# Nine matmuls fewer in batch 0 of a fused attention and MLP kernel, and batch 0's six up-products in one slot

## Chip, cores, metric

One core of a Trainium2 chip. The metric is device microseconds (us) of one execution. The profile of an execution is the record of one such run; its span is some 1.7 us shorter than the time. A difference of 0.1% is 0.3 us here, so the whole case is about tenths of a microsecond in 310.

## The reference

Sliding-window causal attention (8 batches, 8 heads, 576 positions, head size 64, window 64), then a low-rank mix over the positions and a two-layer MLP. Cut to what matters:

```python
rel = pos[:, None] - pos[None, :]
mask = (rel >= 0) & (rel < 64)
attn = softmax(where(mask, q @ k.T / 8, -1e9))      # 8 batches x 8 heads, 576 x 576
x = (attn @ v) -> [8, 576, 512]
u = x + ((x.T @ U) @ V).T                           # U: 576 x 32, V: 32 x 576
out = u + relu(u @ w_ch1) @ w_ch2                   # 512 -> 2048 -> 512, fp32 in and out
```

## The kernel before

Matmuls are bf16. The attention of batch 0 runs first, alone ("prologue"). After that come nine chunks of 512 tokens, each cut into 32 slots: 16 of the first MLP product (tile psA, weights w1b) and 16 of the second (psU, weights w2b). The attention of batches 1 to 7 is cut into pieces that tables place into these slots, so that PE, the tensor engine, never runs dry. `spare` is true for batch 0 alone.

Batch 0's scores, with the product that the change drops: key block 1 against query block 0, where every key lies in the future.

```python
        def SC(j):                       # one head pair
                ...
                scores(banks, 0, j, 0, 0, 2)
                scores(banks, 0, j, 1, 0, 1)
                for u in range(1, NB - 1):
                    scores(banks, u, j, u, u, 2 if u < NB - 2 else 1, last=(u >= NB - 3))
```

The up-products multiply the 64 rank rows (`hh`) by V (`vrep`) into tile psv; the vector engine adds the attention output and so makes u in token-major order:

```python
        def VM(ts, banks=None):          # -> [up, add(0), add(1)]
            def up():
                ...
                for n in range(2):
                    ...
                    nc.tensor.matmul(ps[0][n], vrep[half, off : off + P], hh["sb"][half, lo : lo + cols], start=True, stop=True)
        ...
            pcs["V"] = [f for ts in ((0, 1), (2, 3), (4,)) for f in VM(ts)]     # batch 0
    ...
    DVE_RELU = {0: (7, 9, 11, 15), 1: (3, 6, 8, 9, 10, 12, 13)}
    PLACE_0 = {"V": [0, 0, 1, 2, 2, 3, 4, 4, 4]}
    PLACE_2 = {"S": [8, 8, 8, 11, 11], "M": [8, 9, 10, 12, 13], ...}
```

The first batch is number 0. Batches 2 to 7 get their keys and queries in three steps: GpSimd issues the loads (kr, qr), SyncE (SP) issues ten loads that transpose them (kf, qf) and PE multiplies. Of such a transfer the text names three times: its issue by SP, its landing (the data are there), and its first use. PLACE_2's "S" puts batch 2's scores behind slot 8 of chunk 1. GpSimd waits for a transposed tile before it loads the next batch into the same place:

```python
            def loads(b, *tiles):
                for t in tiles:          # a one-element copy, to wait for transposed tile t
                    nc.gpsimd.tensor_copy(out=held[:], in_=qfs[(b + 1) % 2][0:1, t * HP * P : t * HP * P + 1])
                if b <= 2:
                    load_v(b + 1)
                for _ in load_kq(b + 2, False): pass
            ...
            if b == 1:
                slots[20].append(lambda: loads(1, 2))
```

The prologue begins with matmuls that compute nothing and warm PE up, and has one more of the kind, 512 columns wide, before the third values block:

```python
    turn_over(62, 96)                    # 62 matmuls of 96 columns into an unread bank
    ...
    shift_low(0, nc.scalar.copy, 2)
    a["idle"](1)
    a["PV"][2]()
```

The softmax here doesn't subtract the row's maximum and nothing guards it: scores larger than these inputs give would overflow.

## Time and profile before

| | before |
|---|---|
| time, first 3 runs | 310.14 us (309.88 to 310.33) |
| span of the profiled run | 308.6 us |
| PE busy | 302.1 us, 98% |
| start of the third values block of batch 0 | 16.28 us |
| first psA of chunk 0 | 22.02 us |
| slot 22 of chunk 0 (needs the last quarter of w2b) | 48.45 us, worked out in the prediction |
| first score of batch 2 | 67.59 us |

The lines of the page, the chain and the timeline are in the prediction.

In the chain of waits of before (start, length, what), PE stands still in the middle of the U products:

```profile
19.53 0.32 PE psh L534 x2
19.85 0.31 issue
20.16 0.32 PE psh L543 x4
```

And SP's timeline of before (start, length of the issue, queue, operation, tiles) has the ten transposing loads of batch 2; here the third and the last:

```profile
51.62 1.58 SPq L307 DMA_TRANSPOSE kf<-kr  x1
...
61.52 1.22 SPq L307 DMA_TRANSPOSE qf<-qr  x1
```

The last takes this long to land after its issue:

```profile
DMA to landing us min/median/max: 5.5/5.5/5.5
```

So batch 2's last queries are there at 61.52 + 5.5 = 67.0 (67.06 in the trace), and PE uses them at 67.59. A margin of half a microsecond, as narrow as the ones that the prediction counted at 33, 46 and 48 us.

### The profile page before, as it was taken

What the parts mean: (1) busy time and instruction counts of PE and PEld (TensorE: products, weight loads), DVE (VectorE), ACT (ScalarE), POOL (GpSimd) and SP (SyncE); (2) the same over time, 40 slices, a digit from 0 to 9 for tenths busy, and PEclk for the clock granted to TensorE, in tenths of its full rate; (3) what the DMA queues carried; (4) which work ended last, traced back from release to release, by engine and by line L of the source; (5) the groups of instructions that cost most, each with busy time, mean ns of one, the idle gap of its engine ahead of it and who ended that gap; (6) DMA issues with size and microseconds to landing.
All of it is one profiled execution on the core that took longest, in us unless ns stands there. A gap on an engine that the chain in (4) does not pass through costs nothing.

```text
span 308.6 us, 6947 instructions
## 1 busy us (share of the span) xinstructions
PE 302.1 (98%) x2883; PEld 146.4 (47%) x2883; DVE 174.2 (56%) x336; ACT 106.0 (34%) x169; POOL 102.1 (33%) x136
## 2 busy tenths in 40 slices
PE   7989999999999999999999999999999999999995
PEld 7543454545445544454445444544454444444443
DVE  4585467537848763777467755766576542116012
ACT  2745670358008510552064205430443004101500
POOL 8693264195069519417541725000000000000000
PEclk9999999999999999999999999999999999999999
DMA  7999999999999999999999999955100464010011
GB/s 100 169 208 209 206 172 149 148 139 148 148 108 154 126 158 148 195 161 163 175 176 131 176 175 151 155 111 136 71 2 0 106 229 162 34 68 36 0 68 68
DMA packets 158671, 40.39 MB, mean 131 GB/s; under 512 B 147216, under 2 KB 153616, under 8 KB 158640
## 3 DMA queue, kind: packets, MB, share of 16 engines
q0 software_dynamic: 104720, 18.88, 84.8%
q1 hardware_dynamic: 53920, 21.08, 39.3%
q8 instruction: 22, 0.36, 0.5%
q14 instruction: 9, 0.07, 0.1%
HBM read 37.97 MB, written 9.44 MB: 154 GB/s over the span
## 4 chain that ended last, share of the span: by engine, by line
PE 93%; DMA 3%; POOL 2%; issue 1%; DVE 0%; POOLq 0%
PE psA L766 41%; PE psU L790 41%; DMA vA<-in_v_dram 3%; PE sc L348 3%; PE xw L410 2%; PE psv L661 1%; PE pshh L534 1%; PE tpg L284 0%; POOL qr L121 0%; PE low L348 0%; PE psh L534 0%; POOL vB L153 0%; PE tpu L695 0%; PE xr L410 0%; POOL kr L121 0%
## 5 line engine op out<-in xcount | busy, mean ns | idle before, releaser
L766 PE MATMUL psA<-uTc,w1b 128*128 128x512 bf16 (+1 forms) x580 | 131.0, 378 | 0.3 <-DVE uTc L636 0.3
L790 PE MATMUL psU<-w2b,c 128*128 128x512 bf16 (+2 forms) x592 | 128.4, 374 | 0.0
L790 PEld LDWEIGHTS <-c 128*128 128x128 bf16 x592 | 56.1, 98 | 66.4 <-issue 2.9
L766 PEld LDWEIGHTS <-w1b 128*128 128x128 bf16 x580 | 54.0, 98 | 64.4 <-issue 2.6
L778 ACT ACTIVATE c<-psA 128x512 bf16<-128x512 f32 x84 | 50.1, 597 | 80.5 <-PE psA L766 80.2
L776 DVE TENSOR_SCALAR c<-psA 128x512 bf16<-128x512 f32 x60 | 41.4, 690 | 38.5 <-PE psA L766 38.5
L803 DVE TENSOR_TENSOR osb<-psU,un 128x512 f32<-128x512 f32 (+2 forms) x29 | 19.5, 671 | 51.2 <-PE psU L790 51.2
L368 ACT ACTIVATE pts<-sc 128x1024 bf16<-128x1024 f32 x32 | 31.3, 1030 | 2.8 <-PE sc L348 2.8
L139 POOL DMA_DIRECT2D vA<-in_v_dram x32 | 28.3, 904 | 11.5 <-DMA w1b<-in_moe_w_ch_dram 3.0
L676 DVE TENSOR_TENSOR un<-psv,xs 128x512 bf16<-128x512 f32 (+3 forms) x48 | 25.8, 594 | 6.6 <-PE psv L661 6.5
L130 POOL DMA_DIRECT2D qr<-in_q_dram x30 | 26.6, 887 | 7.0 <-DMA w2b<-in_moe_w_ch_dram 2.9
L130 POOL DMA_DIRECT2D kr<-in_k_dram x30 | 26.3, 876 | 5.0 <-PE psA L766 2.0
L401 ACT ACTIVATE ptl<-low 128x256 bf16<-128x256 f32 x6 | 2.3, 383 | 64.9 <-PE high L348 64.9
L374 DVE TENSOR_TENSOR pts<-pts,maskA 128x1024 bf16<-128x1024 bf16 x28 | 19.0, 683 | 2.2 <-ACT pts L368 2.2
L501 DVE TENSOR_TENSOR xs<-xw,rcw 128x896 bf16<-128x896 f32 x14 | 15.3, 1092 | 0.5
L965 POOL COPY held<-qf 1x1 bf16<-1x1 bf16 x5 | 0.9, 178 | 44.2 <-DMA qf<-qr 44.2
L348 PEld LDWEIGHTS <-kf 64*64 64x64 bf16 x704 | 9.8, 107 | 7.6 <-issue 7.3
L348 PE MATMUL sc<-qf,kf 64*64 64x128 bf16 (+1 forms) x608 | 11.5, 212 | 0.5 <-DVE qf L301 0.3
L410 PEld LDWEIGHTS <-pts 128*64 128x64 bf16 x512 | 10.0, 110 | 3.7 <-issue 3.1
L139 POOL DMA_DIRECT2D vB<-in_v_dram x8 | 7.2, 896 | 5.6 <-DMA qr<-in_q_dram 2.4
L803 DVE TENSOR_TENSOR late<-psU,un 128x512 f32<-128x512 f32 x8 | 5.4, 686 | 6.1 <-PE psU L790 6.1
L410 PE MATMUL xw<-vA,pts 128*64 128x65 bf16 x217 | 8.5, 195 | 0.0
(125 smaller groups left out, 177.1 us busy)
## 6 DMA issues: line engine op xcount, KB each, us to landing
out_dram<-osb SPq DMA_DIRECT2D x27, 256.0 KB, 2.3
vA<-in_v_dram POOLq DMA_DIRECT2D x32, 128.0 KB, 9.6
kr<-in_k_dram POOLq DMA_DIRECT2D x24, 128.0 KB, 7.6
qr<-in_q_dram POOLq DMA_DIRECT2D x24, 128.0 KB, 7.5
w2b<-in_moe_w_ch_dram POOLq DMA_DIRECT2D x4, 512.0 KB, 15.6
out_dram<-late SPq DMA_DIRECT2D x8, 256.0 KB, 3.0
vB<-in_v_dram POOLq DMA_DIRECT2D x8, 128.0 KB, 11.3
w1b<-in_moe_w_ch_dram POOLq DMA_DIRECT2D x2, 512.0 KB, 10.9
```

Of the source, the lines that this page charges most:

```text
L130: nc.gpsimd.dma_start(out=dst[0:rows, t, :, :], in_=src[b, :, t * P : t * P + rows, :].rearrange("h p d -> p h d"),)
L139: nc.gpsimd.dma_start(out=dst[:, :, 0:D], in_=v[b, :, lo : lo + P, :].rearrange("h p d -> p h d"))
L348: nc.tensor.matmul(sc[g][r0 : r0 + W, col * W : (col + n) * W], keys_of(j, u, rs), queries_of(j, blk, n, rs), start=not spare, stop=last o ...
L368: nc.scalar.activation(out=dst, in_=sc[:], func=ACT.Exp, scale=scale)
L374: nc.vector.tensor_tensor(out=dst, in0=dst, in1=maskA.rearrange("p g n w -> p g (n w)"), op=ALU.mult)
L410: nc.tensor.matmul(dst, pts[:, h // 2, h % 2, blk, :] if blk < NB - 1 else ptl[:, h // 2, h % 2, :], rhs, start=True, stop=True,)
L676: nc.vector.tensor_tensor(out=u_tiles[g][rs, cs], in0=ps[0][n][rs], in1=x[rs, t, :, :].rearrange("p h d -> p (h d)")[:, cs], op=ALU.add,)
L766: nc.tensor.matmul(ps[i][:, ts.start * P : ts.stop * P], w1b[:, dc, i * P : (i + 1) * P], uTc[:, ts, dc, :], start=(dc == 0), stop=(dc == ...
L776: nc.vector.tensor_relu(out=c1[i][:], in_=ps[i][:])
L778: nc.scalar.activation(out=c1[i][:], in_=ps[i][:], func=ACT.Relu)
L790: nc.tensor.matmul(acc[t][:, lo:hi], c1[i][:, t * P : (t + 1) * P], w2b[:, i, lo:hi], start=(i == 0), stop=(i == NFC - 1),)
L803: nc.vector.tensor_tensor(out=osb[:, lo:hi], in0=acc[t][:, lo:hi], in1=u_tiles[g][:, lo:hi], op=ALU.add,)
```

## The change

The intent: drop work that cannot matter (eight score products under the mask, one idle matmul), and pay PE's change of array shape once for the six up-products instead of three times.

```diff
-                scores(banks, 0, j, 1, 0, 1)
+                if not spare:
+                    scores(banks, 0, j, 1, 0, 1)
...
-        def idle_turns(n):               # and its users
...
-            pcs["V"] = [f for ts in ((0, 1), (2, 3), (4,)) for f in VM(ts)]
...                                       # two_banks and mixed are now defined for every batch
+        if spare:
+            pcs["V"] = [lambda: mixed([VM((NT - 1,), two_banks), VM((0, 1)), VM((2, 3))])]
...
-    DVE_RELU = {0: (7, 9, 11, 15), 1: (3, 6, 8, 9, 10, 12, 13)}
+    DVE_RELU = {0: (9, 11, 15), 1: (3, 6, 8, 9, 10, 12, 13)}
...
-    PLACE_0 = {"V": [0, 0, 1, 2, 2, 3, 4, 4, 4]}
+    PLACE_0 = {"V": [4]}
...
-    a["idle"](1)
```

Each of the nine matmuls has a weight load beside it: the trace of before shows 2883 of both, 5766 rows of PE's instruction stream. The change takes out 18.

More of the change, by code (lines that the diff above doesn't have):

```diff
@@ L590, in bank @@
             return ua[dc]
-        opened = []
-        def idle_turns(n):
-            cols = P if opened else CH
-            bank(1)
-            for _ in range(n * (CH // cols)):
-                nc.tensor.matmul(
-                    bank(0)[:, 0:cols],
-                    idle[:, 0:P],
-                    idle[:, 0:cols],
-                    start=not opened,
-                    stop=not opened,
-                )
         def XT(t, dcs):
             def f():
-                opened.append(t)
                 for dc in dcs:
@@ L716, in attention, with two_banks, mixed, last @@
             pcs["XT"] = [XT(t, range(NDC if t < 2 else 2)) for t in range(NFULL)]
-            pcs["idle"] = idle_turns
             pcs["X3"] = [XT(t, (2, 3)) for t in (2, 3)]
             pcs["HT"] = [HT((0, 1)), HT((2, 3))]
-            pcs["V"] = [f for ts in ((0, 1), (2, 3), (4,)) for f in VM(ts)]
-        else:
-            def two_banks():
-                return (
-                    psum["mm"].tile([P, CH], FP32, name="psv0", tag="mm"),
-                    ps_tp.tile([P, CH], FP32, name="psv1", tag="tp"),
-                )
-            def mixed(parts=None):
-                parts = parts or [VM((0, 1)), VM((2, 3)), VM((NT - 1,), two_banks)]
-                for part in parts:
-                    part[0]()
-                for part in parts:
-                    for add in part[1:]:
-                        add()
-            pcs["V"] = [mixed]
-            if b == 1:
-                def last():
-                    for f in VM((NT - 1,)):
-                        f()
-                pcs["V"] = [lambda: mixed([VM((0, 1)), VM((2, 3))]), last]
+        def two_banks():
+            return (
+                psum["mm"].tile([P, CH], FP32, name="psv0", tag="mm"),
+                ps_tp.tile([P, CH], FP32, name="psv1", tag="tp"),
+            )
+        def mixed(parts=None):
+            parts = parts or [VM((0, 1)), VM((2, 3)), VM((NT - 1,), two_banks)]
+            for part in parts:
+                part[0]()
+            for part in parts:
+                for add in part[1:]:
+                    add()
+        pcs["V"] = [mixed]
+        if spare:
+            pcs["V"] = [lambda: mixed([VM((NT - 1,), two_banks), VM((0, 1)), VM((2, 3))])]
+        if b == 1:
+            def last():
+                for f in VM((NT - 1,)):
+                    f()
+            pcs["V"] = [lambda: mixed([VM((0, 1)), VM((2, 3))]), last]
+        if not spare:
             pcs["UT"] = [UT(t) for t in range(NT if odd else NT - 1)]
         return pcs
-    DVE_RELU = {0: (7, 9, 11, 15), 1: (3, 6, 8, 9, 10, 12, 13)}
+    DVE_RELU = {0: (9, 11, 15), 1: (3, 6, 8, 9, 10, 12, 13)}
     DVE_RELU_N = (0, 1, 2, 4, 5, 6, 14)
```

## The prediction

> **What bounds the kernel now.** I read the page first, then the chain of waits in order of time, then the timeline around the places that the change touches. The page gives the bound: the tensor engine (PE) is busy for 98% of a span of 308.6 us and makes up 93% of the chain that ended last; the granted clock is full in every slice.
>
> ```profile
> PE 302.1 (98%) x2883; PEld 146.4 (47%) x2883; DVE 174.2 (56%) x336; ACT 106.0 (34%) x169; POOL 102.1 (33%) x136
> PE 93%; DMA 3%; POOL 2%; issue 1%; DVE 0%; POOLq 0%
> ```
>
> A PE at 98% does not say that any matmul taken away is time gained: what counts is whether it stood on the chain. The chain, start and length in us, splits the kernel at 16.28 us.
>
> ```profile
> 6.17 8.05 DMA vA<-in_v_dram
> 14.27 0.61 POOL vB L153
> ...
> 15.61 0.62 POOL vB L153
> 16.28 0.45 PE xr L410 x16
> ...
> 22.02 1.89 PE psA L766 x8
> 23.91 0.32 PE psv L661 x2
> 24.23 0.97 PE psA L766 x4
> 25.20 0.32 PE psv L661 x2
> 25.52 1.83 PE psA L766 x8
> 27.36 0.22 PE psv L661 x2
> 27.57 6.15 PE psA L766 x28
> ...
> 83.25 0.65 PE psv L661 x6
> 83.89 5.29 PE psU L790 x24
> ```
>
> Before 16.28 the chain is not PE at all: the load of batch 0's values has to land, and GpSimd then copies them, half a tile at a time, into the shifted layout vB; the last of its four copies runs 15.61 to 16.22 and releases the third block of attention-times-values. From 22.02 on it is PE without a hole worth the name. So a matmul that ends before 16.28 is free, and one after 22.02 is paid for.
>
> The timeline around 16 us shows one of the matmuls that go, and the wait behind it:
>
> ```profile
> 15.61 0.61 POOL L153 COPY vB<-vA 64x520 bf16<-64x520 bf16 x1
> 15.70 0.39 PE L598 MATMUL uam<-idle 128*128 128x512 bf16 x1
> 16.28 0.19 PE L410 MATMUL xr<-vB,pts 128*64 128x65 bf16 x1 [0.19 <-POOL vB L153]
> ```
>
> The last column is what ended PE's idle time: the copy on GpSimd, not PE's own work.
>
> **What the Trainium skill says.** (1) "TensorE: Matmul & The Clock Gate", section "Wait — 56ns, not 53.3ns?": back-to-back bf16 matmuls of 512 columns start 215.7 ns apart at full clock. The trace agrees: late in the chain, 64 of them take 13.81 us, 215.8 ns each. (2) "TensorEngine Tiling (Array Packing)", section "Key Properties": "Changing tiling mode (not just tile) drains the TensorE". The trace agrees and gives a price: four psA take 0.97 us right behind a psv group, where 4 x 0.2158 = 0.86, so 0.11 us is lost on entering the 128-row shape; 8 take 1.83 against 1.73, and 28 take 6.15 against 6.04: 0.11 us each time. (3) The first page again, section "What's actually happening": the clock is held back only after an idle window of some 3.4 us. Nothing here comes near: with the idle matmul gone, PE would rest from about 15.77 to 16.28, 0.5 us. (4) "PSUM — Partial Sum Buffer", section "The four PSUM rules": a matmul that opens a group overwrites, later ones add. In batch 0 every score bank is opened by the mask bias over all its columns, so leaving out scores that the mask drives to zero still leaves defined sums. This bears on correctness, not on time.
>
> **The change part by part.**
>
> *Eight score matmuls.* For each of four head pairs the product of key block 1 with query block 0 is dropped for two heads: 8 matmuls of 64 columns, wholly under the mask. They lie in groups of 18 that last 0.42 us each with a tail of about 0.2, so one is worth some 0.013 to 0.03 us and all eight 0.1 to 0.25 us of PE time, at 9.6 to 14.2 us. None is on the chain: PE waits there for query copies (0.30 us before 9.60, 0.18 before 12.86) and for the query load that releases the transposes at 11.66, and what is left is swallowed by the wait at 16.28. The vector engine runs nearly back to back from 15.88 and could begin a few hundredths earlier, but its next read is of the block released at 16.28. I count 0.00 us, at best 0.05.
>
> *The idle matmul.* One of 512 columns at 15.70, gone by 16.09, 0.19 us before GpSimd lets PE go on. Removing it lengthens that wait: 0.00 us. It also changes which of two PSUM buffers the first transposes take (the idle one opened the other bank first), but both are free long before the end of the copies.
>
> *The up-products.* Before: three groups of two matmuls (512, 512 and 256 columns) with a 64-row weight tile, in slots 0, 2 and 4 of chunk 0. The two of a group use different row halves and run side by side: 0.32 us is 0.216 + 0.11 to change shape. Each group also makes the following psA pay 0.11. Before, in the chain's numbers: 0.32 + 0.32 + 0.22 for the groups and 3 x 0.11 for the psA behind them, 1.19 us. After: all six stand together at the end of slot 4. This kernel already has such a group in batch 2, with the same six shapes: 0.65 us, then 24 matmuls in 5.29 us where 24 x 0.2158 is 5.18, so 0.11 behind it: 0.76 us. Saving: 1.19 - 0.76 = 0.43 us, all after 22.02 and so on the path.
>
> *What moves with it.* The six additions on the vector engine (four of about 0.645 us and two that take 0.74 together, 3.3 us in all) move from 24.27-28.36 to a block that I estimate at 26.8 to 30.1. The relu of slot 7, on the vector engine at 30.38 before, goes to the scalar engine, which has a 0.92 us hole there; the next relu on the vector engine is slot 9's, whose matmuls end at about 31.6 in the new order. The short up-products now take one of the three buffers that the psA of single slots go round in; slot 7 needs it back at about 29.0 and its additions, placed first, should end at about 27.6. Its transposing bank is needed at slot 11, over 5 us later. I expect no wait from any of these.
>
> Sum: 0.00 + 0.00 - 0.43 = -0.43 us of PE chain.
>
> **The rivals.**
>
> *A load takes the place of the saved time.* If PE comes 0.43 us earlier, it can meet a transfer that is bound by bandwidth and does not move: the DMA stays saturated from 5 to 48 us. The last quarter of the second weight is issued at 36.01 after waiting for the first quarter, and lands at 47.97. Its first reader is in slot 22; the 20 psU from 47.48 are slots 21 to 25, so slot 22 begins at 47.48 + 0.11 + 0.86 = 48.45. The margin is 0.48 us now and would be 0.05 after. Batch 1's query load lands at 33.18 against a first use at 33.93 (0.75 before, 0.32 after), and its last value tile at 46.25 against 46.93 (0.68, 0.25). So the gain just fits. For this rival: a landing 0.2 us later in some executions would cost that much, and the total gain cannot pass about 0.48 us by any route before slot 22. It would make the change -0.2 instead of -0.43, a time of 309.9. I give it a third.
>
> *The score matmuls pay after all.* If scores set the start of the values product by way of the exponentials, 0.1 to 0.2 us more would come: -0.6 us, cut to -0.48 by the load above. Against it: the releaser at 16.28 is GpSimd, whose copies wait for value loads alone. One chance in ten.
>
> *Six matmuls in a row stall, or the late additions do.* The group needs its three pairs of PSUM banks at once; if the bank of slot 2's relu or of the first relu pair came late, PE would stand for some tenths, and if the additions ran into slot 9's relu, slot 12 would wait for its buffer. For it: the order of instructions shows such waits on the first two pairs. Against it: the relus of slots 0 to 2 end by about 25.7 by my count, and the group comes at about 26.5. It would make the change -0.1 to +0.3, up to 310.4. One in ten.
>
> *An unexplained stop moves.* At 19.85 PE stands 0.31 us before the last U product, although the vector engine had written its operand by 19.55; the view calls it issue time. If it depends on where instructions lie in the stream, 18 fewer rows may shift, lengthen or cure it: up to 0.3 us either way, the gain again held at 0.48. I cannot tell from one trace.
>
> **Range and chances.** 310.14 - 0.43 = 309.71; a third of a chance of losing about 0.2 to the load adds some 0.05: I say 309.75 us. The three runs before spread from 309.88 to 310.33, so two medians of three may differ by 0.2 with nothing changed; with about the same again for the size of the effect, 8 in 10 is about 0.4 each way: 309.3 to 310.15. Two per cent is 6.2 us, fourteen times the whole effect, and all three groups together cost 1.19: faster by over 2% 0.01, slower by over 2% 0.01, within 0.98.
>
> **What would show it right or wrong.** Right: the third values block still starts at about 16.3, released by the GpSimd copy after an idle of about 0.5 us; the chain has one psv x6 of about 0.65 us near 26.5, with psA groups before it free of the extra 0.11; slot 22's psU start at about 48.0 without a new wait. Wrong: the 16.28 start comes earlier (the scores counted), a hole before psv or before slots 5 to 7 (banks), psU waiting for the second weight at 48 (the load), or the 0.31 stop gone or grown. The prediction fails as a whole if the time leaves 309.3 to 310.15: below it, something earlier than 16.28 or a stall that I don't see was on the path; above it, one of the new waits is real.

## The result, and the profile after

| | before | after |
|---|---|---|
| runs | 310.32 median of 6 (309.88 to 310.58) | 310.91 median of 6 (310.09 to 311.83) |
| profiled run, span | 308.6 | 308.4 |
| ratio after/before | | 1.002, interval 0.9997 to 1.0043 |

A ratio is the mean time of one kernel's fast runs over that of the other's of the same rounds, so it is not quite the ratio of the medians quoted. Executions over 1.5% slower than the fastest of the same kernel are left out of the means.

The six runs of after are 310.09, 310.16, 310.49 and 311.34, 311.47, 311.83: half like before or a little better, half a whole microsecond worse (the last of them at a mean granted clock of 0.994, the others at 0.999 or 1.000). The median, 310.91, lies outside the predicted range. The profiled run is of the better kind (310.09); keep that in mind for the lines that follow.

The page of after, busy times and the chain's shares (some 20 matmul records are missing in this trace, so PE's busy time is a little low and small "issue" gaps in the chain are not real):

```profile
PE 299.4 (97%) x2853; PEld 145.6 (47%) x2874; DVE 175.0 (57%) x335; ACT 106.6 (35%) x170; POOL 101.9 (33%) x136
PE 91%; DMA 3%; DVE 2%; POOL 2%; issue 1%; POOLq 0%; DVEq 0%
```

New there: DVE, the vector engine, with 2% of the chain, where before had 0%. The chain of after, in order of time, says where:

```profile
6.18 8.01 DMA vA<-in_v_dram
...
15.58 0.62 POOL vB L153
16.25 0.45 PE xr L411 x16
...
19.46 0.32 PE psh L535 x2
19.94 0.44 DVE hh L576
...
21.46 4.48 PE psA L753 x20
25.93 0.65 PE psv L647 x6
26.58 6.15 PE psA L753 x28
...
71.96 0.69 DVE c L763
...
97.31 0.69 DVE c L763
...
101.26 0.39 PE xw L411 x13
```

The third values block starts at 16.25, behind the same GpSimd copy (16.28 before). The stop of 0.31 us in the U products is gone; the first psA comes at 21.46 instead of 22.02. The six psv stand together, 0.65 us, and the 28 psA behind them take 6.15 us, the same as before: no stall. At 71.96 and 97.31 the chain leaves PE for the vector engine (c is a relu's output; the copies into vB stand between them and the values product at 101.26).

With matching weight loads of the two traces set side by side, after's lead over before is: 0.03 us at 16.3, 0.57 at 20.4, **0.99 at 27.6** (behind the six psv), 0.89 at 34, **0.70 at 48.3**, **0.54 at 76**, **0.23 at 102.6**, 0.18 from 143.5 to the end. So even in this run of the better kind the change gains 1 us and four fifths of it are given back, in four places: behind batch 1's query load (landed at 32.97, used at 33.02), the last quarter of w2b (48), and twice behind values products that wait for the vector engine (76, 101). What makes half the runs lose is not in this trace. That was the question for the experiments.

### The profile page after: what moved, and what is told of

Read it like the earlier page. It is cut to its first block, busy times and chain, and to the rows that moved or that the text cites. A ratio compares the mean times of both kernels' runs of the same rounds, so it can differ in the third digit from the quotient of the medians.

```text
span 308.4 us, 6907 instructions
## 1 busy us (share of the span) xinstructions
PE 299.4 (97%) x2853; PEld 145.6 (47%) x2874; DVE 175.0 (57%) x335; ACT 106.6 (35%) x170; POOL 101.9 (33%) x136
## 4 chain that ended last, share of the span: by engine, by line
PE 91%; DMA 3%; DVE 2%; POOL 2%; issue 1%; POOLq 0%; DVEq 0%
PE psU L777 40%; PE psA L753 39%; DMA vA<-in_v_dram 3%; PE sc L348 3%; PE xw L411 2%; PE psv L647 1%; DVE c L763 1%; PE pshh L535 1%; DVE pts L375 1%; PE tpg L284 0%; POOL qr L121 0%; PE low L348 0%; PE psh L535 0%; POOL vB L153 0%; PE tpu L681 0%
## 5 line engine op out<-in xcount | busy, mean ns | idle before, releaser
L777 PE MATMUL psU<-w2b,c 128*128 128x512 bf16 (+2 forms) x573 | 127.1, 373 | 1.2 <-issue 0.3
L763 DVE TENSOR_SCALAR c<-psA 128x512 bf16<-128x512 f32 x59 | 40.7, 689 | 37.2 <-PE psA L753 37.2
```

Of the source, the lines that this page charges most:

```text
L763: nc.vector.tensor_relu(out=c1[i][:], in_=ps[i][:])
L777: nc.tensor.matmul(acc[t][:, lo:hi], c1[i][:, t * P : (t + 1) * P], w2b[:, i, lo:hi], start=(i == 0), stop=(i == NFC - 1),)
```

## The experiments

Five calls, each on one chip with its own runs of before beside it. All results were correct. The medians of before in the calls were 310.46, 310.60, 310.49, 310.50 and 310.33 (7 to 11 runs). In what follows "the slower kind" is a run above 310.95 at a mean granted clock of 0.998 or more; the line was drawn after the runs were seen. The theories by their names in the expectations: **H**, the clock (without the nine matmuls PE is granted its full clock less often); the walls, transfers that don't come earlier when PE does; and **R**, the rows (it matters not what the nine matmuls do but that PE's instruction stream is 18 rows shorter). Where another name stands, what it expects tells which of these it is.

### First call: the parts, each alone

**after_again**: the changed kernel, unedited.

> The changed kernel once more, for the spread and the granted clock of each run. In the first set its six runs ranged from 310.09 to 311.83 us, and the 311.83 one had a mean clock of 0.994. Theory H (clock): in some executions the lighter start lets the clock be held back for one stretch; then again some runs above 311 us, and those show a clock clearly below 1.000. Theory C (copies and loads): the lead won early is lost when the vector engine's copies of vA meet GpSimd's issuing of loads; then runs above 311 us appear with a clock of 1.000 too. Theory N (noise of one set): all runs within 309.9 to 310.6 now.

Measured: 309.89, 310.07, 310.11, 311.41, 311.92 and one of 784.85; ratio 0.9995 (0.9956 to 1.0034). In the last, psA took 823 ns each instead of 378. Its trace holds no record of the clock (the 1.000 listed for it stands for that). The two kinds are there again.

**v_only**: before with nothing but the up-products' move and relu 7.

```diff
-            pcs["V"] = [f for ts in ((0, 1), (2, 3), (4,)) for f in VM(ts)]
+            pcs["V"] = [lambda: mixed([VM((NT - 1,), two_banks), VM((0, 1)), VM((2, 3))])]
-    DVE_RELU = {0: (7, 9, 11, 15), ...
+    DVE_RELU = {0: (9, 11, 15), ...
-    PLACE_0 = {"V": [0, 0, 1, 2, 2, 3, 4, 4, 4]}
+    PLACE_0 = {"V": [4]}
```

> The kernel before with only the up-products moved to one slot; the 8 score matmuls and the idle matmul stay. Theory H: no run with a clock below 0.999, times tight (within 0.6 us), 0.0 to 0.4 us faster than before. Theory C: the lead of about 0.43 us is lost partly or wholly by 105 us, as in the changed kernel; times spread as there.

Measured: 309.80 to 310.54, median 310.13, none of the slower kind in 6; ratio 0.9978 (0.9947 to 1.0009).

**no9**: before with nothing but the nine matmuls gone.

```diff
+                if not spare:
-                scores(banks, 0, j, 1, 0, 1)
+                    scores(banks, 0, j, 1, 0, 1)
-    a["idle"](1)
```

> The kernel before without the 9 matmuls, the up-products left in three slots. Theory H: as in the changed kernel some runs 1 us or more above the rest with a clock below 0.999, mean 0.3 to 0.6 us slower than before. Theory C: the early lead is only what the stop at 19.85 us gives back (0.3 us or more, if it is gone here too), so less is lost and times are near those of before, within 0.2 us. My prediction's view of these matmuls (free, off the chain): same time as before within 0.1 us.

Measured: 310.10 to 310.85, median 310.49, none of the slower kind in 6; ratio 0.999 (0.9956 to 1.0024).

**aft_idle**: after with the idle matmul put back.

```diff
+    a["idle"](1)
     a["PV"][2]()
```

> The changed kernel with the one idle matmul of 512 columns back, the 8 score matmuls still gone. Theory H: if that matmul is what kept the clock, no run with a clock below 0.999 and times of 309.7 to 310.2; if the scores matter as well, fewer slow runs but some. Theory C: spread and mean as in the changed kernel, 310.9.

Measured: one run of 619.1 with psA at 671 ns (no clock record either, left out), the others 310.33 to 310.91; ratio 0.9997 (0.9963 to 1.003).

What follows: neither part alone showed the slower kind, but six runs of each are few, and aft_idle, which has both parts but for one matmul, did not show it in five runs either. The clock does not explain it: after's slow runs mostly have a clock of 1.000, and the two clearly held runs of this call, 312.70 and 312.77 at 0.993 and 0.995, are before's own. Theory H fell here.

These two held runs also stand in the ratios of this call. Without them the mean of before is 310.33, and the plain ratios of the means become 0.9994 for v_only, 1.0005 for no9, 1.0012 for aft_idle and 1.0011 for after_again: all nearer to 1.

### Second call: work or rows, and two more looks at after

**less9**: before with nine of the warm-up matmuls fewer, and the nine disputed ones kept. The stream is 18 rows shorter, the prologue's arithmetic untouched.

```diff
-    turn_over(62, 96)
+    turn_over(53, 96)
```

> The kernel before with 53 instead of 62 of the opening matmuls on zeros (0 to 6 us, read by nobody), nothing else: PE's stream is 18 rows shorter ahead of the last U product, all 9 disputed matmuls stay. In the trace of before PE stands 0.31 us ahead of that product (0.56 us against the spacing of the changed kernel, where it follows in 0.14 us), in the trace of v_only 0.10 (0.35), each time starting 1.4 us after a 16 KB packet of the instruction queue ended; in the changed kernel and in no9 the stop is gone. Theory F (the stop is PE waiting for its own instructions, at a fixed row of the stream): the stop is gone here too, the last U product follows the one before within 0.2 us, and the first psA starts 0.4 to 0.6 us earlier than in before. Theory S (the 9 matmuls themselves hold something up): the stop stays at 0.1 to 0.3 us.

Measured: 310.77 to 311.31, ratio 1.0008 (0.9986 to 1.0029). The time decides nothing. The stop in the U products is gone, but PE came late to it (the last U product at 20.19, the first psA at 22.12, against 22.02 in before), so theory F's gain of 0.4 to 0.6 us is not there to be seen. What the trace does show, about another place, stands below.

**no9_plus9**: no9 with nine matmuls of 8 columns put at the very beginning. Nine disputed matmuls gone, rows as before.

```diff
+    turn_over(9, 8)
     turn_over(62, 96)
```

> no9 with 9 matmuls of 8 columns on zeros put ahead of the opening ones, so that PE's rows stand again where they stood in before, without the 9 disputed matmuls. Theory F: the stop ahead of the last U product is back, 0.3 to 0.6 us against a spacing of 0.14, and the first psA starts 0.3 us or more later than in no9. Theory S: the stop stays away and the first psA starts within 0.1 us of that in no9.

Measured: 310.52 to 311.11, ratio 0.9998 (0.9973 to 1.0022). No stop, but PE was late here too (20.42).

Now SP's timelines. In after, the sixth transposing load of batch 2 is the long one, and the last is issued 0.41 us later than in before although the first was issued earlier:

```profile
51.19 1.23 SPq L307 DMA_TRANSPOSE kf<-kr  x1
...
55.28 2.62 SPq L307 DMA_TRANSPOSE qf<-qr  x1
...
61.93 1.22 SPq L307 DMA_TRANSPOSE qf<-qr  x1
```

In less9, too, the lengthened ones are at 55 to 57, with all nine disputed matmuls in place:

```profile
55.20 1.78 SPq L307 DMA_TRANSPOSE qf<-qr  x1
57.08 1.96 SPq L307 DMA_TRANSPOSE kf<-kr  x1
```

In no9_plus9, without those nine but with the rows, it is the third again, as in before:

```profile
51.40 1.86 SPq L307 DMA_TRANSPOSE kf<-kr  x1
```

What lies under it is a transfer of the kind "instruction", one packet of 16,384 bytes. The DMA view of before between 51 and 53 us (kind: packets, MB, share of the engines):

```profile
q8 instruction: 1, 0.02, 3.0%
```

and of after between 55 and 57 us; neither kernel has one in the other's window:

```profile
q8 instruction: 1, 0.02, 5.4%
```

The packets next to it move little (45.77 in before, 45.40 in after; 71.07 and 70.37), this one from 51.81 to 55.28. So theory R holds for the traces: the number of rows moves the packet, whichever matmuls are taken out, and the load that it falls on is long in issue, which delays those behind it. Not all of a long issue is the packet's: the sixth load took 1.57 us in before, with no such packet there.

Set against PE's own work, the place of the packet is sharper than by the clock time. In all nine undisturbed traces of the short stream it starts 0.08 to 0.72 us after the first of PE's transposes of u (tile tpu, 55.04 in after); in all eight of the long stream it starts 3.36 to 4.91 us before it.

**after_look1**, **after_look2**: the changed kernel, to catch the slower kind in a trace.

> The changed kernel, one look, for a trace of the slower of its two kinds of runs: of 11 runs outside the 784.85 us one, 6 took 309.9 to 310.5 and 5 took 311.3 to 311.9 us, four of these at a clock of 0.999 or 1.000. If this look is of the slower kind, its lead over before should be the same 0.9 us or more at 45 us and be lost by 1.3 us more than in the first trace at one place; theory L (loads): at a wait of PE for the second weight or for values, between 40 and 105 us; theory V (vector engine): at the up-products or the values products, behind slow vector copies; theory K: all along, by a lower clock. If it is of the faster kind it tells nothing new.

> A second such look at the changed kernel; the same expectation as for the first: the slower kind of run in about 45 of 100 looks.

Measured: 311.44 and 311.13, both the slower kind. The waits of PE in after_look2 between 66 and 69 us (line, what for: us in all, times, longest):

```profile
PE low L348 <- DMA qf<-qr: 1.2, 1, 1.2
```

That is batch 2's first score, waiting for the last transposed queries. These landed late, by the view of that one load, issued at 61.90:

```profile
DMA to landing us min/median/max: 6.2/6.2/6.2
```

In after's own trace the same load, issued at 61.93, needed 4.9 us and was there at 66.8, just before PE came at 66.90.

In after_look2 PE led before by 1.07 us at 27.6 and 0.69 at 48; behind this wait it was 0.59 *behind* before, and 0.85 behind at the end. after_look1 lost elsewhere: it had started 1.1 us late at 14 to 17, was 0.19 behind from 27.6 to 120, and then stood 0.8 us for batch 4's queries at 126, which landed at 127.32.

So a lead is not only taken back by a wall; the lead can turn into a loss. But there is more than one wall, and PE need not be early to meet one: after_look1 was behind before when it stood at 126.

### Third call: is it the first scores' place?

**after_s9** puts batch 2's scores one slot (0.9 us) later, so that the load is not waited for; **before_s9** is its control. **before_s7** puts before's scores one slot earlier, which makes before use them as early as after does.

```diff
 # after_s9, before_s9 (before_s7 has 7,7,7 and 7,8,9)
     PLACE_2 = {
-        "S": [8, 8, 8, 11, 11],
-        "M": [8, 9, 10, 12, 13],
+        "S": [9, 9, 9, 11, 11],
+        "M": [9, 10, 11, 12, 13],
```

> The changed kernel with batch 2's scores one slot later in chunk 1 (slot 9 in place of 8, masks moved with them). Why: in the second look at the changed kernel PE came to these scores at 66.9 us and stood until 68.18, 0.04 us after the last transposed load of batch 2's queries had landed at 68.14; in its first trace that load landed at 66.83 and PE passed without a wait. Theory T (that load is the wall: PE gains nothing by coming before about 67 to 68 us): PE now comes at about 67.8, the wait is at most 0.4 us, the slower kind of run (311.3 to 311.9 at full clock) is gone, median 309.8 to 310.2, 0.1 to 0.5 us faster than before. Rival V (vector copies behind the values products at 75 and 101 us decide): nothing gained, or 0.3 us lost as masks come later; median 310.8 with the same spread.

Measured: 310.02 to 311.62, median 310.54, ratio 1.0004 (0.9986 to 1.0022). A miss: 309.8 to 310.2 had been expected. In its trace the queries landed at 68.65, later than in any other, and PE waited 0.45 us for them even in the later slot.

> The kernel before with batch 2's scores one slot later, as a control of the move itself: PE comes at about 68.5. Theory T: median within 0.2 us of before, and no run at full clock above 310.8. If the move itself costs (masks later, values products wait at 75 us), it is 0.2 to 0.5 us slower, and that much has to be taken off what after_s9 shows.

Measured: 309.91 to 310.98, median 310.19, ratio 0.9992 (0.9974 to 1.0009).

> The kernel before with batch 2's scores one slot earlier (slot 7 in place of 8), all 9 matmuls and the three-slot up-products in place. PE comes to these scores at about 66.7 us, as early as in the changed kernel. Theory T: the slower kind of run appears in a kernel that has none of the change: some or most runs 0.6 to 1.3 us above before, median 310.6 to 311.6, and the trace shows PE waiting for the load of qf by the transposing queue ahead of the scores. Rival (the slower kind comes from the change's own parts, banks or additions): median within 0.15 us of before, no such wait.

Measured: 309.99 to 311.20, median 310.83, ratio 1.0006 (0.9989 to 1.0022). In its trace the queries landed at 66.26, PE came at 66.38 and had no wait. The median is what theory T expected, but one run of six is of the slower kind and the expected wait was not seen: not decided.

**no9_plus9_b** is the same kernel as no9_plus9, once more for the stop in the U products at 19.85.

> no9_plus9 once more, since in its first look PE came to the last U product only at 20.41 us, later than the time at which its rows were to be expected (the instruction packet ended at 18.90, and 1.43 us later is 20.33). Theory F: if PE comes early this time (the U product before it at 19.4 to 19.8), it stands again until 1.4 us after the packet's end, 0.2 to 0.6 us; if PE is late again it tells nothing.

Measured: 311.44 at a clock of 0.998, and no stop; PE came late into that stretch in both, so they say nothing of it.

### Fourth call: take the company away from the late load

With `loads(1, 3)` GpSimd waits for one transposed tile more before it issues the next values and keys, so that those loads start later and the last transposing load no longer runs beside them.

```diff
-                slots[20].append(lambda: loads(1, 2))
+                slots[20].append(lambda: loads(1, 3))
```

**after_hold3**:

> The changed kernel, with GpSimd holding back the loads of the next batches until the transposed queries of tile 3 of batch 2 have landed, not tile 2. In the traces the last transposed load (tile 4) shares the DMA engines with those value loads and takes 4.9 to 6.4 us from issue to landing (66.3 to 68.7 us), where such loads without that company take 2.4 us. Theory T: it now lands by about 65, PE at 66.9 never waits for it, the slower kind of run is gone (none above 310.8 at full clock), median 309.7 to 310.2, 0.5 to 1.0 us below after_again2. Rival V (later waits behind vector copies take it all back): median within 0.3 us of after_again2, runs above 311 remain.

Measured: 311.10 to 311.46, median 311.26, ratio 1.0022 (1.0007 to 1.0038): a miss in the time. The load itself did what was meant:

```profile
DMA to landing us min/median/max: 2.6/2.6/2.6
```

It landed at 64.56, and PE had no wait at 67. But in the timeline of after_hold3 PE now stands at the first psA of chunk 2:

```profile
92.22 0.38 PE L753 MATMUL psA<-uTc,w1b 128*128 128x512 bf16 x1 [0.84 <-DVE late L790]
```

The releaser that the view names had long been done. It was a transposing load of chunk 2's u, landed at 91.97: SP issued those from 88.20 on, behind batch 3's ten, against 85.82 in before. In this run the wall at 67 was moved to 92, not removed.

**v_only_hold3**, **before_hold3**: the same edit in v_only and in before.

> The up-products alone in one slot, plus the hold; the 9 matmuls stay. Theory T: 309.7 to 310.1, 0.3 to 0.5 us faster than before, all runs within 0.6 us: the up-products' 0.43 us kept for the most part. Rival V: like v_only, 0.1 to 0.3 us faster than before.

Measured: 310.32 to 311.51, median 310.98, ratio 1.0015 (0.9995 to 1.0035); queries landed at 63.85.

> The kernel before with the same hold. PE comes to batch 2's scores at 67.6, in most runs after the landing, so theory T: 0.0 to 0.3 us faster than before, with fewer runs above 310.8. If the hold itself costs (value loads 1.8 us later), it shows here: up to 0.5 us slower.

Measured: 310.03 to 311.45, median 310.91, ratio 1.0008 (0.9987 to 1.0028); landed at 64.04. Three runs of each are of the slower kind, though the nine matmuls are in; before without the edit had 2 of 11 in this call. So the slower kind does not need the short stream, and what the edit gains at 67 can't be read from these times.

**after_again2**: the changed kernel once more, for the count.

> The changed kernel once more, beside after_hold3 on the same chip. Theory T: the slower kind again in about half of the runs, median 310.3 to 311.4; if the trace is of that kind, it shows PE's wait for qf ahead of the scores at 67 to 68 us (or at 126 us, as in the first look).

Measured: 309.99, 310.06, 310.63, 310.73, 311.32 (clock 0.994), 311.44; ratio 1.0004 (0.9984 to 1.0024).

### Fifth call: rows alone

**after_plus9**: after with the rows given back (`turn_over(9, 8)` first, as in no9_plus9).

> The changed kernel with 9 matmuls of 8 columns on zeros put at the very start, so that PE's stream has as many rows as before. Theory R (rows): an instruction packet at 51 to 52 us, none at 55 to 57; the ten transposed loads of batch 2 issued over 12.6 to 12.7 us, the last one about 0.8 us earlier than in the changed kernel; the slower kind of run gone (at most one of six above 310.9 at full clock), median 309.8 to 310.3, at or below before. Theory M (the 9 matmuls or the earlier PE itself): packet and issue as in the changed kernel, slower kind in about half of the runs, median 310.5 to 311.4.

Measured: 309.50, 309.66, 310.55, 310.74, 311.02 and, in the profiled run, 313.27 at a clock of 0.989; ratio 0.9999 (0.998 to 1.0017). Not decided. In that trace the clock was at half from 12.1 to 18.9 us and PE 2 us late everywhere; the packet came at 54.80 and the ten issues took 13.36 us. Its rows are those of before, so R had expected the early packet, at 51 to 52 us. By the clock time that failed; by PE's work it did not: PE came to its first tpu at 57.73 here, and the packet started 2.93 us before that, on the side of the long stream. So PE's lateness goes with the late packet, and the trace speaks for R rather than against it. Of the times, R's median (309.8 to 310.3) was missed.

**v_less9**: v_only with nine warm-up matmuls fewer (`turn_over(53, 96)`): the up-products' gain and the short stream, the disputed nine kept.

> v_only with 53 instead of 62 opening matmuls: the 9 disputed matmuls are there, the rows are as few as in the changed kernel. Theory R: it behaves as the changed kernel does: packet at 55 to 57 us, ten transposed loads issued over 13.3 to 13.5 us, the slower kind (above 310.9) in two to four of six runs, median 310.4 to 311.4. Theory M: it behaves as v_only: 12.6 us, no run above 310.9, median 310.0 to 310.4.

Measured: 310.25 to 311.18, median 310.78, one of the slower kind in 5 (R had expected two to four of six; its median fits); ratio 1.0014 (1.0000 to 1.0027). The trace is as R expected. SP's timeline of v_only:

```profile
51.49 1.63 SPq L307 DMA_TRANSPOSE kf<-kr  x1
```

and of v_less9, which differs by nine idle matmuls at the start:

```profile
55.49 2.62 SPq L307 DMA_TRANSPOSE qf<-qr  x1
```

All traces in one table, but for those of the two slow runs (784.85 and 619.1). Ten issues: from the start of the first to the start of the last of batch 2's transposing loads. Landing: the last of them.

| rows | traces | packet, us | ten issues, us | landing, us |
|---|---|---|---|---|
| 5766 | before, v_only, no9_plus9 (2), before_s7, before_s9 | 51.38 to 51.86 | 12.60 to 12.65 | 66.26 to 67.06 (4 of the 6 known) |
| 5766, held clock | after_plus9 | 54.80 | 13.36 | 67.46 |
| 5748 | no9, after (4), less9, after_s9, v_less9 | 55.12 to 56.64 | 13.36 to 13.49 | 66.83 to 68.65 (7 of the 8 known) |
| 5766, one load later | before_hold3, v_only_hold3 | 51.25, 52.07 | 12.64, 12.67 | 63.85, 64.04 |
| 5748, one load later | after_hold3 | 55.40 | 13.37 | 64.56 |

The mean landing of the first row is 66.65, of the third 67.6. All runs of one kernel, at a clock of 0.998 or more: before 55 runs, mean 310.46, 7 of the slower kind; after 17 runs, mean 310.73, 7 of the slower kind; v_only 6 runs, mean 310.15, none. So 7 of 17 against 7 of 55. Over all kernels without the holding edit it is 11 of 42 with the short stream and 12 of 83 with the long one: the short stream alone does not separate the two kinds.

## Why the prediction was wrong, step by step

**"Saving: 1.19 - 0.76 = 0.43 us, all after 22.02 and so on the path."** Right. The lead grows by 0.42 us from 20.4 to 27.6, the group takes 0.65 us and the psA behind it lose 0.11 as worked out.

**Scores and idle matmul, 0.00 us.** Right as to their work: the start at 16.28 moved by 0.03, and no9 alone is at 310.49 against 310.46. The start itself is no fixed point: in three traces of after it is 16.17, 16.25 and 16.79, each time behind the GpSimd copy, a spread larger than the forecast gain. In the fourth, after_look1, it is 16.96, and there PE itself was late: it had waited 1.13 us for batch 0's queries, until 12.78, and went through its scores without a stop up to the values. In such a run the scores do stand on the chain. Also right: no stall before the six psv, none behind the additions.

**"If it depends on where instructions lie in the stream, 18 fewer rows may shift, lengthen or cure it".** The stop at 19.85 was cured in after, for 0.5 us of lead, which the sum did not have. No trace with 5748 rows has it. But among the eight with 5766 the last U product comes late by 0.56 us in before, 0.35 in v_only, 0.10 and 0.03 in before_s7 and before_s9, and not at all in the other four: before's trace was an unlucky one of its kind, and the cause stays open.

**"Sum: 0.00 + 0.00 - 0.43 = -0.43 us of PE chain", and then 310.14 - 0.43.** This is the step that failed. It took a chain that was PE without a hole as one that stays so when PE comes earlier. The prediction looked for walls, with the right means, but only among the loads up to 48 us, and let the rival end as a cap ("the total gain cannot pass about 0.48 us by any route before slot 22"). That cap was itself off: the last quarter of w2b landed at 47.55 instead of 47.97, and slot 22 began right behind it, at 47.59, so 0.70 us of lead passed. The places after it were not looked for. They are:

- 67 us, batch 2's transposed queries: there at 67.06 for a use at 67.59 in before. With PE 0.7 us early the margin is used up, before anything else changes.
- 76 and 101 us, values products behind copies on the vector engine, which cost the lead 0.16 and 0.31 us; the one at 101 met runs whether early or late (see below).
- 92 us, chunk 2's transposed u: there at 90.89 for a use at 91.83 in before.
- 126 us, batch 4's queries, seen as a wait of 0.8 us in after_look1 and of 0.14 in v_only_hold3.

The rival that was given a third was sized "-0.2 instead of -0.43". What the runs show is a gain of 0.2 us left in the one traced run of the better kind, and a loss of about 1 in 7 of 17 runs.

**The second failure: the nine matmuls counted as free.** They are free as work and not free as rows. With 18 rows fewer the instruction packet of 51.5 us falls at 55.5, on another load of the same ten, and takes longer there (0.97 us in before, 1.72 in after, by its record). The ten take 0.8 us more and the last lands, in the mean, 0.95 us later, just where the margin was half a microsecond. less9 and v_less9 show it without removing the nine, no9_plus9 shows its absence without keeping them. Here the Trainium skill would have helped, had it been looked up: "Runtime: NRT & Kernel Launch", section "Instruction fetch mechanics", says that engines refill their program in blocks of 16 KiB, 256 instructions, over a DMA queue of their own. The trace agrees: 22 packets, 16,384 bytes each, and 5766 rows / 256 = 22.5. The same section calls the cost "mostly hidden"; at this place it was not.

**The vector engine's part.** Its timeline around 99 us. Before:

```profile
97.85 0.69 DVE L776 TENSOR_SCALAR c<-psA 128x512 bf16<-128x512 f32 x1 [0.79 <-PE psA L766]
...
99.66 0.28 DVE L153 COPY vB<-vA 64x520 bf16<-64x520 bf16 x1
```

After:

```profile
97.31 0.69 DVE L763 TENSOR_SCALAR c<-psA 128x512 bf16<-128x512 f32 x1 [0.79 <-PE psA L753]
...
99.12 0.69 DVE L153 COPY vB<-vA 64x520 bf16<-64x520 bf16 x1
```

It starts 0.54 us earlier, just as PE does, and loses 0.41 of it in one copy that takes 0.69 instead of 0.28. GpSimd issues loads throughout in both. The Trainium skill, "SBUF — State Buffer", section "Who interferes with whom", says that the vector engine's fast copy and GpSimd share a pair of ports that one of them holds for the whole instruction while the other blocks. That fits, and which of the two came first would then depend on tenths of a microsecond; no run here isolates it.

The other kept traces settle how often this happens, and that being early is not what brings it. In the six (before, before_s7, before_hold3, after_look1, after_s9, v_less9) in which all the copies around 100 us take 0.35 us or less, PE loses nothing there. In the other twelve the longest takes 0.47 to 0.79, and each of these traces loses 0.2 to 0.76 us against before at this place: no9_plus9 0.45 and less9 0.36, both behind before when they came, and v_only 0.26. So before's trace was a lucky one here, as it was an unlucky one at 19.85, and this loss is a part of the spread of both kernels, not a price of the change.

**The chances.** 0.98 for "within 2%" was right, and easy, as the prediction says itself: the ratio is 1.002.

What is shown and what is not. Shown: the gain up to 27.6 us in one trace; the places where the lead is given back in it; the shift by rows and the later issue in undisturbed traces; the waits of 1.2 and 0.8 us in two runs of the slower kind; that in one run of the holding edit a wait at 92 took the place of that at 67. Supported, not shown: that the rows make the slower kind more frequent (v_only 310.15 with 0 of 6, v_less9 310.72 with 1 of 4 at full clock, but in different calls, on one chip; no9 and aft_idle, with the short stream, had 0 of 6 and 0 of 5; after_s9 and after_plus9 missed what this theory expected of their times). Open: why a packet at 55 us takes longer than at 51.5, why 18 rows put it behind the start of tpu, 3.5 us later, while its neighbours keep their places, and which wait catches a run. So the failed step is shown, but the cause of the slower median is shown only in part. No version was shown to beat both kernels: v_only comes nearest, at 0.9978 of before, or 0.9994 without the two held runs, with an interval (0.9947 to 1.0009) that includes 1.

## What to carry to other kernels

When a change makes the bounding engine arrive earlier, list every operand that comes by a transfer over the *whole* kernel, with its landing and its first use, and take the smallest margin as the gain that can last; a margin of 0.5 us in one trace is nothing if that landing varies by more than a microsecond from run to run. Instructions that cost no time are not nothing in a stream that is itself loaded by DMA: removing 18 rows moved a refill by 3.5 us. And look at the single runs: two kinds of run a microsecond apart are a better clue than a median between them. A single trace of each kernel is not enough to tell a stop of the kernel from a stop of that run: here before's one trace had a stop at 19.85 that four of its kind did not have, and lacked one at 101 that twelve of eighteen had.

## What the Trainium skill lacked or had wrong

- "Runtime: NRT & Kernel Launch", section "Instruction fetch mechanics": right about the block of 16 KiB (22 packets of 16,384 bytes). It calls the cost of a block boundary "mostly hidden" and says nothing of loads in flight at that time: a transposing load on which the refill fell was 2.62 us in issue instead of 1.22, and the last of the ten was issued 13.4 us after the first or 12.6, depending on where it fell.
- "TensorEngine Tiling (Array Packing)", section "Key Properties": states that a change of array shape drains, but no price; here 0.11 us each.
- "TensorE: Matmul & The Clock Gate", section "What's actually happening": the table there ties a held clock to an idle window of about 3.4 us. That does not cover what one run shows: in after_plus9 the clock was at half from 12.1 to 18.9 us, and the longest stand of PE up to then was 1.3 us (11.33 to 12.62). Before itself had runs of 312.70 and 312.77 at mean clocks of 0.993 and 0.995, not traced.
- "SBUF — State Buffer", section "Who interferes with whom": has no duration for such a copy; the same 64 x 520 copy took 0.28 and 0.69 us here with GpSimd issuing loads beside it (consistent with it, not isolated).
- No page that I read gives the spread of a landing: the same transposing load took 4.9, 5.5 and 6.2 us beside the loads of the next batches and 2.6 us without them.
